# Attention on one core: transposes of q, k and the log rows in the half-array form of the scores, and one PSUM slot for both halves of the product with v

## The chip, the cores and the metric

One core of a Trainium2 chip runs the whole program. The metric is the device time of one launch in microseconds (us), taken as the median of repeated runs. The core has five engines with queues of their own: PE (TensorE, matrix products), DVE (VectorE), ACT (ScalarE), POOL (GpSimd) and SP, which here only starts transfers. Products land in PSUM, which DVE and ACT read; POOL can't. All data of the attention are single precision; a number is split into a high part of type fp32r and the rest, and products are made of the parts.

## What is computed

The reference chains an attention with decay and two expert layers. The change lies in the attention alone:

```python
B, H, S, D = q.shape                     # 4, 8, 576, 64
scores = scale * np.matmul(q, k.transpose(0, 1, 3, 2))
log_f = np.log(np.clip(f, 0.0001, 1.0))
cum = np.cumsum(log_f, axis=-1)
decay = cum[:, :, :, None] - cum[:, :, None, :]
scores = np.where(causal, -1000000000.0, scores + decay)
attn = np.exp(scores - np.max(scores, axis=-1, keepdims=True))
attn = attn / (np.sum(attn, axis=-1, keepdims=True) + 1e-09)
x = np.matmul(attn, v)                   # then moe (w_in, w_out), then moe2 (gate, w1, w2)
```

## The kernel before

**Stages.** The first stage is the attention of 32 heads, worked as 16 pairs of heads; weights of w_in are loaded and converted beside it. Then come the products with w_in and w_out (`h`, `acc`), the routing, and eight experts (`h`, `y`). The stage of attention runs from the start to the first product `h<-X,wh`.

**One pair.** `prepare` loads q and k of a pair (tiles `x3`, and `x4` for the last 64 tokens), transposes them on PE into a PSUM tile `s`, and ACT and DVE make the high parts (`qh`, `kh`) and low parts (`ql`, `kl`); here lines 636 to 665. `offsets` multiplies all parts for scores with queries along the partitions, finds each row's minimum of the negated scores (DVE, `kept`, `nm`), sums the exponentials (ACT, `sm`), makes the logarithm of the sums (ACT, then a series on POOL, tile `ln`) and turns maximum plus logarithm into rows by a transpose (`rows`, line 676; ACT and DVE split it, tile `xr`; SP carries it into `qr`). `attend` multiplies again with keys along the partitions, takes exponentials that are then final (`P`), zeroes what is not causal (POOL, `affine_select`), multiplies with v in two halves of the queries (`values`, 320 and 256 columns) and stores the result as high and low parts (`finish`, tile `xt`).

**Forms of PE.** The products of the scores use rows 0 to 63 for one head and rows 64 to 127 for the other, side by side ("64*128" in the rows). Products with v use columns in two halves ("128*64"). Transposes and the products with the weights use the whole array ("128*128").

**Who sets the order.** `Plan` holds every operation with its engine, an assumed length in ns, what it needs, a rank, and the buffers that it takes; `order` runs through the plan as a list of events and so fixes the order of each engine. The ranks are `12 * n` plus constants (`ZP`, `ZO`, `ZA`, `ZS`, `ZH`, `ZL`, `ZR`) and a table by pair (`ZN`, `ZM`, `ZB`). On PE it looks for another ready operation of the same `form` (within `NEAR` ranks) before it changes form, which it counts with `TURN` (200 ns). PSUM has four slots `s` (`SB`), each of two banks of 512 words. All operations recorded so have line 72 in the profile.

Of the kernel before, what the change touches and what calls it, by code (L numbers as in the profile page):

```python
# [37 lines left out]
ZX = 500  # L38
ZP, ZO, ZA, ZH, ZL, ZW, DW = -39, -27, 5, -9.5, -10.5, 63, 14.5
ZS = 5, 5.5, 7, 0.5, 2.5, 11, 11.5  # L40
ZQ = 1
ZT = 0, 7
ZR = 5.5
MW = 1.5, 0.6
# [6 lines left out]
NEARB = 5  # L51
ZN = 0.5, 0, -4, 0, 0, 0, -0.5, 0, 0, 0, 0, 0, 0, 0, 2, 0.5
ZM = -2.5, -0.5, 0, -1, 0, 0, 0, 0, 0, 0, 0, 1, -1.5, 0.5, 4, -4
ZB = 0, -4, -5, 0, 0, 0.5, -0.5, 0, 0, -3, 0, -4, 0.5, 0, 0, -1
NK = 4
# [36 lines left out]
class Plan:  # L92
# [4 lines left out]
           ("vec", "act"): 205, ("vec", "gp"): 155, ("act", "gp"): 180}  # L97
    MOVE = 650, 2600
    TURN = 200
# [4 lines left out]

    def op(self, eng, ns, fn, needs=(), rank=0.0, takes=(), uses=(), move=0, plain=False, form="A"):
        o = Op(eng, ns, fn, [x for x in needs if x is not None], rank)
        o.move, o.form = move, form
# [12 lines left out]
        self.ops.append(o)  # L120
        return o
# [4 lines left out]
    def order(self):  # L126
# [100 lines left out]
def tile_kernel(ctx, tc, q, k, v, f, w_in, w_out, w_gate, w1, w2, out):  # L227
# [35 lines left out]
    def weight_ops(op, pieces, z, st, low_on, keep=None, hold=()):  # L263
# [7 lines left out]
        def chunk(c, src):  # L271
# [32 lines left out]
            wb = o.got[0]  # L304
            s = op("gp", 800, square, [o], z, ["wsq"], [wb])
            sq = s.got[0]
# [3 lines left out]
            o = op("vec", 335, b2, [o], z, (), [bb, wb])  # L310
            s = op("gp", 816, big, [s], z, (), [sq])
            takes = [] if "b" in st else ["wst"]
            o = op("gp", 687, mul, [s, o] + st.get("o", []), z, takes, [sq, bb] + ([st["b"]] if "b" in st else []))
            if takes:
# [198 lines left out]
    with ExitStack() as c1:  # L513
# [63 lines left out]
        QO = stp.tile([128, 128], FR, name="qo")  # L577
        VT = [stp.tile([128, 5, 2, D], FT, name=f"vt{i}") for i in range(2)]
        pads = []
        for n in range(NS):  # L580
# [16 lines left out]
            if n < 2:  # L597
                op("gp", 150, lambda n=n: gp.memset(VT[n][64:, 4], 0.0), (), 12 * n - 90)
        marks, users = [], []
        heads = [(b, hp) for b in range(B) for hp in range(H // 2)]  # L600

        def prepare(n, own, z):
# [30 lines left out]
            def part(end, z):  # L633
                mine = {}

                def flip():
                    mine[0] = p = bank()
                    if end:
                        pe.transpose(p[:, 0, :128], x3["end"].rearrange("p s d -> p (s d)"), ident)
                        return  # L640
                    for j in range(2):
                        for t in range(4):
                            pe.transpose(p[:, j, 128 * t:128 * t + 128], x3[j][:, t].rearrange("p s d -> p (s d)"), ident)

                def high(j, c0, w, a):
                    hi = (qh[:, 64:] if j else kh)[:, c0:c0 + w]
                    x = mine[0][:, 0, a:a + w] if end else mine[0][:, j]
                    if j:
# [4 lines left out]
                def low(j, c0, w, a):  # L653
                    hi, lo = ((y[:, 64:] if j else y)[:, c0:c0 + w] for y in ((qh, ql) if j else (kh, kl)))
                    x = mine[0][:, 0, a:a + w] if end else mine[0][:, j]
                    vec.scalar_tensor_tensor(lo, x, 0.125 if j else 1.0, hi, op0=OP.mult, op1=OP.subtract)
                if end:
                    o = op("pe", 109, flip, loads["end"], z, ["s"], buf["end"] + list(sets.values()))
# [4 lines left out]
                for j, c0, w, a in ([(0, 512, 64, 0), (1, 512, 64, 64)] if end else [(0, 0, 512, 0), (1, 0, 512, 0)]):  # L663
                    a_ = op("act", 51 + .833 * w, lambda x=(j, c0, w, a): high(*x), [o], z + ZH, (), [tb, sets[j]])
                    outs[j] += [a_, op("vec", 69 + 1.042 * w, lambda x=(j, c0, w, a): low(*x), [a_], z + ZL, (), [tb, sets[j]])]
            part(False, z)
# [9 lines left out]
        def rows(x, dst, need, z, uses, duse):  # L676
# [3 lines left out]
            def flip():  # L680
                mine[0] = bank()[:10, 0, :128]
                pe.transpose(mine[0], x(), ident)

            def high():
                mine[1] = at.tile([10, 2, 128], FR, name="xr", tag="xr", bufs=2)
                act.copy(mine[1][:, 0], mine[0])

            def low():
                vec.tensor_tensor(mine[1][:, 1], mine[0], mine[1][:, 0], op=OP.subtract)
            o = op("pe", 107, flip, need, z + 1, ["s"], uses)  # L690
            st = o.got[0]
# [5 lines left out]
        def offsets(n, own, z):  # L697
# [70 lines left out]
            def ratio():  # L768
                own["ln"] = x = at.tile([128, 4, 10], FT, name="ln", tag="ln", bufs=2)
                act.activation(x[:, 0], own["sm"].bitcast(I32), AF.Copy, scale=LN[0], bias=LN[1])  # L770
                act.activation(x[:, 1], x[:, 0], AF.Exp)

            def ready():
                x = own["ln"]
                gp.tensor_scalar(x[:, 3], own["sm"], 1e-9, None, op0=OP.add)

            def series():
                x, t = own["ln"][:, 2], own["ln"][:, 1]
                gp.tensor_tensor(t, own["ln"][:, 3], t, op=OP.mult)
                gp.tensor_scalar(x, t, LN[5], LN[4], op0=OP.mult, op1=OP.add)  # L780
# [3 lines left out]
                gp.tensor_scalar(x, x, LN[2], None, op0=OP.add)  # L784
                gp.tensor_tensor(x, x, own["ln"][:, 0], op=OP.add)
# [3 lines left out]
            p = op("gp", 250, ready, tots + [o], z + ZR, (), [sb, lb])  # L789
            o = op("gp", 2200, series, [o, p], z + ZR, (), [nb, sb, lb])  # L790
            own["max"] = rows(lambda: own["ln"][:, 2], lambda l: qr[32 + l:97 + l:64], [o], z + ZR, [lb], kq)

        def attend(n, own, z):
# [18 lines left out]
            def score(name, blocks, z):  # L812
# [24 lines left out]
                for n, (i, f0, f1) in enumerate(blocks):  # L837
                    sel = []
                    if f0 == 128 * i:
                        w = min(128, f1 - f0)  # L840
                        sel = [op("gp", 137 + 1.75 * w, lambda a=col[n], w=w: causal(a, w), acts, z + 4, (), [pb])]
                    for half, (q0, w) in enumerate(HALF):
# [4 lines left out]
            def values(half, i, z):  # L847
                need, pb, name, a, e, x, y = W[half, i]

                def product():  # L850
                    if i == 0:
                        own["av", half] = bank()[:, 0]
                    for u in range(2):
                        pe.matmul(own["av", half][64 * u:64 * u + 64, x:y], own["v"][:, i, u], own["P", name][:, u, a:e],
                                  start=i == 0, stop=i == (2, 4)[half])
                o = op("pe", 4 * (e - a) / 2.4 + 12, product, need + vl + R.get(("av", half), []), z, ["s"] if i == 0 else [],
                       [vb, pb] + R.get(("avb", half), []), form="V")
                if i == 0:
                    R["avb", half] = [o.got[0]]
                R["av", half] = [o]  # L860

            def finish(half, z):
# [22 lines left out]
                if rest == "gp":  # L885
                    o = op("gp", 96 + 3.55 * w, lambda: low(1), [o], z + 1, (), [xb])
                    o = op("gp", 148 + 2.1 * w, lambda: low(0), [o], z + 1, (), [xb])
                else:
# [534 lines left out]
```

## Time and profile before

| | before |
|---|---|
| median of 3 runs (lowest, highest) | 925.02 us (924.19, 928.3) |
| profiled execution, its span | 927.42 us, 925.7 us |
| busy: PE, DVE, ACT, POOL | 889.4, 584.0, 416.6, 457.6 us |
| from 40 to 180 us: PE, DVE, ACT, POOL | 137.07, 103.50, 130.83, 108.47 us |
| granted clock of PE over the span | 0.989 |

Busy time of PE counts the modelled ends of pipelined products, so lengths of PE are read from start to start. A row of the timeline merges alike instructions ("x8") and gives the start of the first. A wait is put down to the engine whose signal came last.

### The profile page before, as it was taken

The numbers are of one execution on the slowest core, as the hardware profiler recorded it, in microseconds if no ns is written. First come the engines' busy times: TensorE is split into PE (matmuls) and PEld (weight loads), VectorE is DVE, ScalarE is ACT, GpSimd is POOL, SyncE is SP. The second block draws the span as 40 slices with busy tenths as digits, with TensorE's granted clock in tenths as the row PEclk, the third lists the DMA queues.
The fourth block names the chain that finished last, engine by engine and source line by source line (L and its number), as shares of the span: only waits on it lengthen the run. The fifth ranks groups of instructions, "written<-read, shape, count | busy, mean of one in ns | idle before, by whom it ended". The sixth has DMA issues, their size and how long they took to land.

```text
span 925.7 us, 19093 instructions
## 1 busy us (share of the span) xinstructions
PE 889.4 (96%) x6934; PEld 755.8 (82%) x6934; DVE 584.0 (63%) x1439; ACT 416.6 (45%) x983; POOL 457.6 (49%) x683
## 2 busy tenths in 40 slices
PE   6899999998999999999999999999899999999996
PEld 6688878876877787777777777777689999999996
DVE  8778876517798389323576677766755665556631
ACT  7899999842222233223122222222344555455521
POOL 8588895548997078000645655555662122121101
PEclk9899999999999999999899999999999999999999
DMA  6566654559984384321312212211246765656611
GB/s 128 149 163 172 182 138 120 178 148 339 323 281 148 137 261 134 114 82 46 124 48 70 69 46 69 69 58 58 80 163 190 225 189 177 196 186 194 189 38 35
DMA packets 139967, 132.36 MB, mean 143 GB/s; under 512 B 68480, under 2 KB 106688, under 8 KB 139872
## 3 DMA queue, kind: packets, MB, share of 16 engines
q1 hardware_dynamic: 135600, 121.40, 42.5%
q0 software_dynamic: 3072, 9.44, 3.5%
q8 instruction: 55, 0.90, 0.4%
q10 hardware_dynamic: 1200, 0.30, 0.1%
q14 instruction: 40, 0.33, 0.1%
HBM read 99.84 MB, written 31.08 MB: 141 GB/s over the span
## 4 chain that ended last, share of the span: by engine, by line
PE 69%; issue 11%; POOL 10%; DVE 4%; ACT 2%; DMA 2%; SPq 0%; POOLq 0%; DVEq 0%; ACTq 0%
PE acc L1059 21%; PE h L72 19%; PE s L72 9%; PE h L1141 6%; PE y L1154 6%; POOL wsq L72 3%; PE T L72 3%; PE q_ct L1059 2%; POOL wst L72 2%; POOL ln L72 1%; ACT kept L72 1%; DVE r_ge L1301 1%; DVE kept L72 1%; POOL P L72 1%; POOL out L1162 1%
## 5 line engine op out<-in xcount | busy, mean ns | idle before, releaser
L72 PE MATMUL h<-X,wh 128*128 128x512 f32 (+1 forms) x960 | 209.6, 375 | 0.6 <-DVE xt L72 0.6
L72 PEld LDWEIGHTS h<-X,wh 128*128 128x128 f32 x960 | 165.0, 188 | 37.8 <-DVE g L72 2.7
L1059 PE MATMUL acc<-wh,gh 128*128 128x512 f32 x576 | 188.2, 404 | 0.0
L453 POOL TENSOR_TENSOR gl<-g,gh 128x512 fp32r<-128x512 f32 x64 | 104.9, 1643 | 82.7 <-ACT gh L452 73.9
L1059 PEld LDWEIGHTS acc<-wh,gh 128*128 128x128 f32 x576 | 108.1, 192 | 19.3
L359 ACT CAST wh<-wst 128x512 fp32r<-128x512 f32 x132 | 80.4, 621 | 84.6 <-DMA wst<-in_moe_w 49.4
L1059 PE MATMUL acc<-wh,gl 128*128 128x512 f32 x288 | 117.4, 408 | 0.9 <-POOL gl L453 0.9
L1141 PE MATMUL h<-XE,wh 128*128 128x288 f32 x768 | 116.7, 301 | 0.9 <-DVE XE L1003 0.9
L72 DVE TENSOR_TENSOR wh<-wst,wh 128x512 fp32r<-128x512 f32 x132 | 91.2, 713 | 40.3 <-ACT wh L359 28.1
L452 ACT CAST gh<-g 128x512 fp32r<-128x512 f32 x72 | 44.5, 621 | 155.0 <-PE acc L1059 132.5
L72 ACT ACTIVATE g<-h 128x512 f32<-128x512 f32 (+1 forms) x80 | 44.4, 555 | 154.4 <-PE h L72 154.4
L1141 PEld LDWEIGHTS h<-XE,wh 128*128 128x128 f32 x768 | 105.3, 189 | 1.2 <-DVE XE L1003 1.2
L1154 PE MATMUL y<-eh,wh 128*128 128x288 f32 x512 | 98.3, 296 | 0.0
L72 DVE TENSOR_TENSOR g<-g,h 128x512 f32<-128x512 f32 (+1 forms) x80 | 50.2, 629 | 68.6 <-ACT g L72 68.2
L72 ACT ACTIVATE kept<-kept,nm 128x192 f32<-128x192 f32 (+4 forms) x160 | 88.0, 553 | 2.9 <-DVE nm L72 2.9
L1162 POOL DMA_INDIRECT out<-yo,ids x24 | 24.8, 1034 | 127.0 <-DVE yo L1161 117.9
L1154 PEld LDWEIGHTS y<-eh,wh 128*128 128x128 f32 x512 | 79.7, 188 | 0.0
L72 DVE SCALAR_TENSOR_TENSOR wbits<-w,wbits 128x256 int32<-128x256 int32 x128 | 76.2, 597 | 3.0
L72 DVE CUSTOM_DVE_ANT_0 kept<-s,mask 128x192 f32<-128x192 f32 (+4 forms) x160 | 59.2, 426 | 23.0 <-PE s L72 22.5
L1154 PE MATMUL y<-el,wh 128*128 128x288 f32 x256 | 68.2, 296 | 0.0
L72 POOL TENSOR_TENSOR wst<-wsq,wbits 128x256 f32<-128x256 f32 x64 | 49.6, 775 | 36.4 <-DVE wbits L72 31.5
L1059 PEld LDWEIGHTS acc<-wh,gl 128*128 128x128 f32 x288 | 55.3, 192 | 10.9 <-POOL gl L453 1.3
(228 smaller groups left out, 1594.9 us busy)
## 6 DMA issues: line engine op xcount, KB each, us to landing
wst<-in_moe_w SPq DMA_DIRECT2D x128, 256.0 KB
X<-xd SPq DMA_DIRECT2D x12, 1024.0 KB
g<-gd SPq DMA_DIRECT2D x36, 256.0 KB
w<-in_moe_w_in SPq DMA_DIRECT2D x32, 256.0 KB
w<-in_moe_w_out SPq DMA_DIRECT2D x32, 256.0 KB
gd<-g SPq DMA_DIRECT2D x16, 512.0 KB
xd<-xt SPq DMA_DIRECT2D x16, 320.0 KB
x2d<-xo SPq DMA_DIRECT2D x20, 256.0 KB
```

The source lines that it names most:

```text
L72: r = getattr(self.engine, name)(*a, **k)
L359: A.copy(r[u][0], x)
L452: A.copy(gh, g)
L453: on.tensor_tensor(gl, g, gh, op=OP.subtract)
L1059: tc.keep_in_program_order(PE.matmul(*a, **k))
L1141: PE.matmul(h[:, :CAP], w, X[:, c, x, :], start=n == 0, stop=n == 3 * NC - 1)
L1154: PE.matmul(yt[c][:, :CAP], w[:, s], a, start=j == 0 and n == 0, stop=j == NJ - 1 and n == 2)
L1162: sd = G.indirect_dma_start(out=out[:, :], out_offset=bass.IndirectOffsetOnAxis(ap=ids[:, 3 * e + t:3 * e + t + 1], axis=0), in_=y, in_off ...
L1301: V.scalar_tensor_tensor(many[:, :NT * (K + 1)].rearrange("p (i k) -> p i k", k=K + 1)[:, :, :K], key[:, :, None].to_broadcast(s), base if ...
```

## The change

q and k are loaded with four neighbouring tokens in each partition, and each transpose is made in two halves of 64 rows by 64 columns which write two banks of the slot; the rows of ln likewise, from a wider zeroed tile. Such transposes have the scores' form `S`, and `pull=False` keeps the plan from drawing them forward for the sake of the form. Each copy and subtraction of q and k now reads both banks, so the two copies (q first) and the two subtractions follow each other. The halves of the product with v take the two banks of one slot. The first half's result is copied by DVE instead of ACT (`FIN`). The ranks, the tables by pair and some assumed lengths have other numbers.

```diff
-ZP, ZO, ZA, ZH, ZL, ZW, DW = -39, -27, 5, -9.5, -10.5, 63, 14.5
+ZP, ZO, ZA, ZH, ZL, ZW, DW = -43.5, -24.5, 7, -3.5, -8.5, 61.5, 23.5
...
-FIN = ("act", "vec"), ("vec", "gp")
+FIN = ("vec", "vec"), ("vec", "gp")
...
-    MOVE = 650, 2600
+    MOVE = 650, 2200
...
-                    same = [x for x in q if x[2].form == form and x[0] <= q[0][0] + self.near]
+                    same = [x for x in q if x[2].form == form and x[0] <= q[0][0] + self.near * x[2].pull]
...
+        lnt = [stp.tile([128, 160], FT, name=f"ln{i}") for i in range(2)]
+        LNS = [{0: x[:, 0:10], 1: x[:, 10:20], 3: x[:, 20:30], 2: x[:, 32:42], 4: x[:, 32:160]} for x in lnt]
...
-                at_q[j].dma_start(x3[j][:, :, i], src[b, h + i, :512].rearrange("(t p) d -> p t d", p=128))
+                at_q[j].dma_start(x3[j][:, :, i], src[b, h + i, :512].rearrange("(p t) d -> p t d", t=4))
...
-                    for j in range(2):
-                        for t in range(4):
-                            pe.transpose(p[:, j, 128 * t:128 * t + 128], x3[j][:, t].rearrange("p s d -> p (s d)"), ident)
+                    for j, t in [(0, 0)] if end else [(j, t) for j in range(2) for t in range(4)]:
+                        for r in range(2):
+                            d = slice(64 * r, 64 * r + 64)
+                            if end:
+                                pe.transpose(p[:, r, :64], x3["end"][d].rearrange("p s d -> p (s d)"), ident[d, d])
+                            else:
+                                pe.transpose(p[:, r, 4 * j + t::8], x3[j][d, t].rearrange("p s d -> p (s d)"), ident[d, d])
...
+                    return mine[0].rearrange("p r (c n) -> p (r c) n", n=8)[:, :, 4 * j:4 * j + 4]
...
-                    o = op("pe", 872, flip, loads[0] + loads[1], z, ["s", "k", "q"], buf[0] + buf[1])
+                    o = op("pe", 888, flip, loads[0] + loads[1], z, ["s", "k", "q"], buf[0] + buf[1], form="S", pull=False)
...
+                for j in (1, 0):
+                    need = [o] if end or j else [o, a_[1]]
+                    a_[j] = op("act", 51 + .833 * w, lambda x=(j, c0, w, 0): high(*x), need, z + ZH, (), [tb, sets[j]])
+                for j in range(2):
+                    need = [a_[j]] if end else list(a_.values())
...
                 def product():
+                    if i == 0 and half == 0:
+                        own["avs"] = bank()
                     if i == 0:
-                        own["av", half] = bank()[:, 0]
+                        own["av", half] = own["avs"][:, half]
```

On PE, around one product with v in the middle of the stage, stood before (`x_112` and `x_113` are k and q of a later pair, `x_2331` their last 64 tokens):

```order
L72 MATMUL s<-kl_132,qh_128 128x288 x2
L72 MATMUL s<-kr_133,qo 128x288 x2
L72 MATMUL s<-ident,ln 10x128
L72 MATMUL s<-ident,x_112 128x128 x4
L72 MATMUL s<-ident,x_113 128x128 x4
L72 MATMUL s<-P,vt_135 64x320 x2
L72 MATMUL s<-P,vt_135 64x192 x2
L72 MATMUL s<-P,vt_135 64x64 x2
L72 MATMUL s<-P,vt_135 64x256 x6
L72 MATMUL s<-P,vt_135 64x192 x2
L72 MATMUL s<-P,vt_135 64x64 x2
L72 MATMUL s<-ident,x_2331 128x128
```

The same place on PE, with the change:

```order
L72 MATMUL s<-kl_132,qh_128 128x288 x2
L72 MATMUL s<-kr_133,qo 128x288 x2
L72 MATMUL s<-P,vt_135 64x320 x2
L72 MATMUL s<-P,vt_135 64x192 x2
L72 MATMUL s<-P,vt_135 64x64 x2
L72 MATMUL s<-P,vt_135 64x256 x6
L72 MATMUL s<-P,vt_135 64x192 x2
L72 MATMUL s<-P,vt_135 64x64 x2
L72 MATMUL s<-ident,x_2379 128x64 x2
L72 MATMUL s<-ident,ln_137 128x64 x2
L72 MATMUL s<-qh_116,kh_119 128x320 x2
```

The transposes of k and q have gone from between the scores and v into the scores before (they stand some rows further up), the one of ln behind v, and no instruction of the whole array is left.

On POOL, between the store of one pair's result (`xt`) and the selects of the next (`AFFINE_SELECT`), stood before, in one of these places:

```order
L72 TENSOR_SCALAR ln<-sm 128x10
L72 TENSOR_SCALAR xt<-xt 128x256
L72 TENSOR_TENSOR ln<-ln 128x10
L72 TENSOR_SCALAR ln<-ln 128x10
L72 TENSOR_TENSOR ln<-ln 128x10
L72 TENSOR_SCALAR ln<-ln 128x10
L72 TENSOR_TENSOR ln<-ln 128x10
L72 TENSOR_SCALAR ln<-ln 128x10
L72 TENSOR_TENSOR ln<-ln 128x10
L72 TENSOR_TENSOR ln<-ln,nm 128x10
L72 TENSOR_TENSOR xt<-xt 128x256
L72 AFFINE_SELECT P<-P 128x2x128
```

and with the change:

```order
L72 TENSOR_SCALAR xt<-xt 128x256
L72 TENSOR_SCALAR ln_137<-sm 128x10
L72 TENSOR_TENSOR xt<-xt 128x256
L72 AFFINE_SELECT P<-P 128x2x128
L72 TENSOR_TENSOR ln_137<-ln_137 128x10
L72 TENSOR_SCALAR ln_137<-ln_137 128x10
L72 TENSOR_TENSOR ln_137<-ln_137 128x10
L72 TENSOR_SCALAR ln_137<-ln_137 128x10
```

The first select of a pair, on which its product with v waits, has moved ahead of the series for ln.

## Rows read from the trace of the kernel before

**Rows 1.** The page: busy time by engine, and its DMA line.

```profile
PE 889.4 (96%) x6934; PEld 755.8 (82%) x6934; DVE 584.0 (63%) x1439; ACT 416.6 (45%) x983; POOL 457.6 (49%) x683
DMA packets 139967, 132.36 MB, mean 143 GB/s; under 512 B 68480, under 2 KB 106688, under 8 KB 139872
```

**Rows 2.** Busy time by stretches, with the columns' names first.

```profile
core 0: us, PE busy (x) PEld busy (x) DVE busy (x) ACT busy (x) POOL busy (x), PEclk, DMA share, GB/s
27.60:30.90 3.30, 3.21 (x24) 3.20 (x25) 2.73 (x15) 3.30 (x15) 1.27 (x6) 0.50 0.59 132
41.20:44.50 3.30, 3.30 (x22) 2.09 (x20) 2.64 (x6) 2.28 (x7) 2.22 (x3) 0.50 0.61 138
40.00:180.00 140.00, 137.07 (x1675) 119.70 (x1677) 103.50 (x419) 130.83 (x393) 108.47 (x247) 0.99 0.57 152
```

**Rows 3.** Timeline of PE, one period: start us, us, line, operation, tiles, shape, count.

```profile
144.85 2.94 PE L72 MATMUL s<-P,vt 128*64 128x320 f32 x32
147.72 0.33 PE L72 MATMUL s<-ident,x 128*128 128x128 f32 x1
147.98 0.41 PE L72 MATMUL s<-qh,kh 64*128 64x320 f32 x2
...
152.38 0.28 PE L72 MATMUL s<-kh,ql 64*128 64x64 f32 x2
152.49 0.28 PE L72 MATMUL s<-kl,qh 64*128 64x64 f32 x2
...
154.52 0.29 PE L72 MATMUL s<-kl,qh 64*128 64x288 f32 x2
154.65 0.29 PE L72 MATMUL s<-kr,qo 64*128 64x288 f32 x2
154.88 0.28 PE L72 MATMUL s<-ident,ln 128*10 128x128 f32 x1
154.99 1.04 PE L72 MATMUL s<-ident,x 128*128 128x128 f32 x8
155.95 0.76 PE L72 MATMUL s<-P,vt 128*64 128x320 f32 x4
```

**Rows 4.** Timeline of PE near the end of the stage.

```profile
191.59 0.28 PE L72 MATMUL s<-qr,kr 64*128 64x64 f32 x2
191.80 2.96 PE L72 MATMUL s<-P,vt 128*64 128x320 f32 x32
194.69 0.41 PE L72 MATMUL s<-qh,kh 64*128 64x320 f32 x2
```

**Rows 5.** PE's waits, 10 to 40 us, then 40 to 202: total, times, longest.

```profile
PE s L72 <- DVE nm L72: 1.9, 4, 1.1
...
PE s L72 <- DVE xr L72: 2.0, 1, 2.0
PE s L72 <- POOL P L72: 1.7, 3, 1.3
```

**Rows 6.** Groups by shape, 0 to 202 us: busy us, mean ns; idle before, releaser.

```profile
L72 ACT ACTIVATE qh<-s 128x512 fp32r<-128x512 f32 x12 | 7.0, 585 | 0.0
L72 ACT CAST xt<-s 128x320 fp32r<-128x320 f32 x16 | 6.5, 408 | 2.7 <-PE s L72 2.7
...
L72 DVE SCALAR_TENSOR_TENSOR kl<-s,kh 128x512 fp32r<-128x512 f32 x12 | 8.3, 690 | 9.3 <-ACT qh L72 9.3
L72 DVE TENSOR_TENSOR xt<-s,xt 128x320 fp32r<-128x320 f32 x16 | 7.8, 485 | 9.8 <-ACT xt L72 9.8
L72 DVE COPY xt<-s 128x256 f32<-128x256 f32 x16 | 6.7, 418 | 3.6 <-PE s L72 3.1 <-issue 0.4
L72 DVE TENSOR_SCALAR wbits<-w 128x256 int32<-128x256 int32 x16 | 5.9, 367 | 4.4 <-DMA w<-in_moe_w_in 2.9 <-POOL wst L72 1.4
```

**Rows 7.** Timelines where attention ends, PE and POOL.

```profile
201.70 11.50 PE L72 MATMUL h<-X,wh 128*128 128x512 f32 x48 [0.58 <-DVE xt L72]
...
209.92 0.72 POOL L72 TENSOR_TENSOR wsq<-w 128x256 f32<-128x256 f32 x1 [6.52 <-DMA w<-in_moe_w_out]
```

More of the change, by code (lines that the diff above doesn't have):

```diff
@@ L103, in __init__, with op @@
         self.near, self.linger = near, linger
-    def op(self, eng, ns, fn, needs=(), rank=0.0, takes=(), uses=(), move=0, plain=False, form="A"):
+    def op(self, eng, ns, fn, needs=(), rank=0.0, takes=(), uses=(), move=0, plain=False, form="A", pull=True):
         o = Op(eng, ns, fn, [x for x in needs if x is not None], rank)
-        o.move, o.form = move, form
+        o.move, o.form, o.pull = move, form, pull
         for t in takes:
@@ L304, in chunk @@
             wb = o.got[0]
-            s = op("gp", 800, square, [o], z, ["wsq"], [wb])
+            s = op("gp", 665, square, [o], z, ["wsq"], [wb])
             sq = s.got[0]
@@ L310, in chunk @@
             o = op("vec", 335, b2, [o], z, (), [bb, wb])
-            s = op("gp", 816, big, [s], z, (), [sq])
+            s = op("gp", 875, big, [s], z, (), [sq])
             takes = [] if "b" in st else ["wst"]
-            o = op("gp", 687, mul, [s, o] + st.get("o", []), z, takes, [sq, bb] + ([st["b"]] if "b" in st else []))
+            o = op("gp", 740, mul, [s, o] + st.get("o", []), z, takes, [sq, bb] + ([st["b"]] if "b" in st else []))
             if takes:
@@ L637, in flip, with turned, like @@
                     mine[0] = p = bank()
-                    if end:
-                        pe.transpose(p[:, 0, :128], x3["end"].rearrange("p s d -> p (s d)"), ident)
-                        return
-                    for j in range(2):
-                        for t in range(4):
-                            pe.transpose(p[:, j, 128 * t:128 * t + 128], x3[j][:, t].rearrange("p s d -> p (s d)"), ident)
+                    for j, t in [(0, 0)] if end else [(j, t) for j in range(2) for t in range(4)]:
[5 more added lines that the diff above has]
+                                pe.transpose(p[:, r, 4 * j + t::8], x3[j][d, t].rearrange("p s d -> p (s d)"), ident[d, d])
+                def turned(j):
+                    if end:
+                        return mine[0][:, j, :64]
+                    return mine[0].rearrange("p r (c n) -> p (r c) n", n=8)[:, :, 4 * j:4 * j + 4]
+                def like(x):
+                    return x if end else x.rearrange("p (c t) -> p c t", t=4)
                 def high(j, c0, w, a):
-                    hi = (qh[:, 64:] if j else kh)[:, c0:c0 + w]
-                    x = mine[0][:, 0, a:a + w] if end else mine[0][:, j]
+                    hi, x = like((qh[:, 64:] if j else kh)[:, c0:c0 + w]), turned(j)
                     if j:
@@ L653, in low @@
                 def low(j, c0, w, a):
-                    hi, lo = ((y[:, 64:] if j else y)[:, c0:c0 + w] for y in ((qh, ql) if j else (kh, kl)))
-                    x = mine[0][:, 0, a:a + w] if end else mine[0][:, j]
+                    hi, lo = (like((y[:, 64:] if j else y)[:, c0:c0 + w]) for y in ((qh, ql) if j else (kh, kl)))
+                    x = turned(j)
                     vec.scalar_tensor_tensor(lo, x, 0.125 if j else 1.0, hi, op0=OP.mult, op1=OP.subtract)
                 if end:
-                    o = op("pe", 109, flip, loads["end"], z, ["s"], buf["end"] + list(sets.values()))
+                    o = op("pe", 111, flip, loads["end"], z, ["s"], buf["end"] + list(sets.values()), form="S", pull=False)
                 else:
-                    o = op("pe", 872, flip, loads[0] + loads[1], z, ["s", "k", "q"], buf[0] + buf[1])
+                    o = op("pe", 888, flip, loads[0] + loads[1], z, ["s", "k", "q"], buf[0] + buf[1], form="S", pull=False)
                     sets[0], sets[1] = own["k"], own["q"] = o.got[1:]
                 tb = o.got[0]
-                for j, c0, w, a in ([(0, 512, 64, 0), (1, 512, 64, 64)] if end else [(0, 0, 512, 0), (1, 0, 512, 0)]):
-                    a_ = op("act", 51 + .833 * w, lambda x=(j, c0, w, a): high(*x), [o], z + ZH, (), [tb, sets[j]])
-                    outs[j] += [a_, op("vec", 69 + 1.042 * w, lambda x=(j, c0, w, a): low(*x), [a_], z + ZL, (), [tb, sets[j]])]
+                a_ = {}
+                for j in (1, 0):
+                    c0, w = (512, 64) if end else (0, 512)
+                    need = [o] if end or j else [o, a_[1]]
+                    a_[j] = op("act", 51 + .833 * w, lambda x=(j, c0, w, 0): high(*x), need, z + ZH, (), [tb, sets[j]])
+                for j in range(2):
+                    need = [a_[j]] if end else list(a_.values())
+                    outs[j] += [a_[j], op("vec", 69 + 1.042 * w, lambda x=(j, c0, w, 0): low(*x), need, z + ZL, (), [tb, sets[j]])]
             part(False, z)
@@ L680, in flip @@
             def flip():
-                mine[0] = bank()[:10, 0, :128]
-                pe.transpose(mine[0], x(), ident)
+                p = bank()
+                for r in range(2):
+                    d = slice(64 * r, 64 * r + 64)
+                    pe.transpose(p[:, r, :64], x()[d], ident[d, d])
+                mine[0] = p[:10, :, :64]
             def high():
                 mine[1] = at.tile([10, 2, 128], FR, name="xr", tag="xr", bufs=2)
-                act.copy(mine[1][:, 0], mine[0])
+                act.copy(mine[1][:, 0].rearrange("p (r c) -> p r c", r=2), mine[0])
             def low():
-                vec.tensor_tensor(mine[1][:, 1], mine[0], mine[1][:, 0], op=OP.subtract)
-            o = op("pe", 107, flip, need, z + 1, ["s"], uses)
+                hi, lo = (mine[1][:, l].rearrange("p (r c) -> p r c", r=2) for l in range(2))
+                vec.tensor_tensor(lo, mine[0], hi, op=OP.subtract)
+            o = op("pe", 111, flip, need, z + 1, ["s"], uses, form="S", pull=False)
             st = o.got[0]
@@ L784, in series @@
                 gp.tensor_scalar(x, x, LN[2], None, op0=OP.add)
-                gp.tensor_tensor(x, x, own["ln"][:, 0], op=OP.add)
+                gp.tensor_tensor(x, x, own["ln"][0], op=OP.add)
                 gp.tensor_tensor(x, x, own["nm"][:, :10], op=OP.add)
@@ L788, in offsets @@
             lb = o.got[0]
-            p = op("gp", 250, ready, tots + [o], z + ZR, (), [sb, lb])
-            o = op("gp", 2200, series, [o, p], z + ZR, (), [nb, sb, lb])
-            own["max"] = rows(lambda: own["ln"][:, 2], lambda l: qr[32 + l:97 + l:64], [o], z + ZR, [lb], kq)
+            p = op("gp", 285, ready, tots + [o], z + ZR, (), [sb, lb])
+            o = op("gp", 1760, series, [o, p], z + ZR, (), [nb, sb, lb])
+            own["max"] = rows(lambda: own["ln"][4], lambda l: qr[32 + l:97 + l:64], [o], z + ZR, [lb], kq)
         def attend(n, own, z):
@@ L840, in score @@
                         w = min(128, f1 - f0)
-                        sel = [op("gp", 137 + 1.75 * w, lambda a=col[n], w=w: causal(a, w), acts, z + 4, (), [pb])]
+                        sel = [op("gp", 200 + 1.68 * w, lambda a=col[n], w=w: causal(a, w), acts, z + 4, (), [pb])]
                     for half, (q0, w) in enumerate(HALF):
@@ L855, in product @@
                                   start=i == 0, stop=i == (2, 4)[half])
[L856 to L859, printed above, removed]
+                o = op("pe", 4 * (e - a) / 2.4 + 12, product, need + vl + R.get(("av", half), R.get("begun", [])), z, ["s"] if i == half == 0 else [],
+                       [vb, pb] + R.get(("avb", 0), []), form="V")
+                if i == half == 0:
+                    R["avb", 0] = R["avb", 1] = [o.got[0]]
+                    R["begun"] = [o]
                 R["av", half] = [o]
```

31 lines of the change are left out of this document (16 added, 15 removed).

## Prediction, made before the changed kernel ran

> **What bounds the kernel now.** I read the page first: PE is busy 96% of the span, ACT, DVE and POOL 45 to 63% [rows 1]. The change sits in the attention stage, which ends with the first product with w_in at 201.7 us [rows 7]; so the second view is the table by stretches of that stage. From 40 to 180 us PE is busy 137.1 of 140 us, ACT 130.8, POOL 108.5, DVE 103.5 [rows 2]: two engines are nearly full at once, PE first. In two stretches, 27.6 to 30.9 and 41.2 to 44.5 us, the granted clock is 0.50, the lower of the two levels (1.2 GHz); both come behind waits of PE for DVE, of 1.1 us at the longest between 10 and 40 us and of 2.0 us just after [rows 2, 5]. The third view is one period of the pipeline on PE, from a product with v to the next, 144.85 to 155.95 us: 11.10 us without a wait [rows 3]. It goes V (products with v), one transpose, scores, nine transposes (one of ln, eight of q and k), V. The fourth is the list of PE's waits, of which the largest are in rows 5. What comes behind the stage hangs on it: the w_out loads stand on SP's queue behind the last stores of attention but one, and POOL waits for them until 209.92 us [rows 7]. So I let what the stage gains pass whole to the end.
>
> **Turns of PE (removed).** The scores use the array as two halves of 64 rows; the transposes of before use all of it (128x128); V uses two halves of columns. By the two orders of PE, up to the first product with w_in, PE changes form 64 times before and 34 times after. What a turn costs is read as start to start [rows 3, 4]. Between score pairs of 64 columns the step is 0.11 us (152.38 to 152.49), of 288 columns 0.13 us (154.52 to 154.65); between whole transposes 0.11 us (154.88 to 154.99).
> - V, one transpose, scores: from the transpose to the first score 0.26 us (147.72 to 147.98). V straight to scores takes as long from V's start to the next instruction as V to the transpose (2.89 us, 191.80 to 194.69, against 2.87 us, 144.85 to 147.72). So a transpose among the scores, at 0.11 us, saves 0.15 us. There are 9 such places: 1.35 us.
> - Scores, transposes, V: from score to transpose 0.23 us where 0.13 is the pace, so 0.10; from the last of eight transposes to V 0.96 - 7 x 0.11 = 0.19, so 0.08 over the pace. Scores straight to V: 0.21 us (191.59 to 191.80), 0.10 over. The saving is 0.10 + 0.08 - 0.10 = 0.08 us, at 12 places: 0.95 us.
> - Scores, transposes, scores: 4 places ahead of the first V, 0.10 + 0.15 = 0.25 us each, 1.0 us. PE waits for others there, so I count half, 0.5 us.
> Together 2.8 us, on the path since PE is 98% busy from 40 to 180 us.
>
> **The transposes themselves.** Each whole one becomes two of 64 rows by 64 columns. The trace has none of that kind; the nearest row is a score pair of 64 columns, which loads the same 64x128 weights twice and takes 0.11 us for both. That is the price of one whole transpose, so the swap costs nothing. The other end: the halves run one behind the other at 0.11 us each, 10 x 0.11 = 1.1 us for each of 16 head pairs, 17.6 us. I take the near row. Output with a stride of 8 words in PSUM, and ACT and DVE reading it in runs of four words, stand in no row; the nearest are DVE's copy of 256 neighbouring words from PSUM at 418 ns and its shift of 256 words of w, every second one, at 367 ns [rows 6]. By them a stride costs nothing, or gains 51 ns; I take nothing, and 51 ns either way for four copies and subtractions in 16 pairs, 3.3 us, as bounds.
>
> **ACT, DVE, POOL.** The copy of the first half of the result moves from ACT (408 ns, x16, 6.5 us) to DVE (about the 485 ns of the subtraction of the same size, 7.8 us) [rows 6]. ACT, 93% busy, becomes lighter by 0.41 us a period; DVE idles 36.5 of 140 us, 3.0 us a period, which hides the copy as long as it isn't at the head of DVE's queue when scores end. The subtraction for k now waits for both copies of ACT, q's first; a full copy is 585 ns. DVE already waits 9.3 us for ACT's copies of q ahead of the 12 subtractions for kl [rows 6], so I take nothing, and 0.59 us a pair, 7 us, as bound. On POOL the first causal select of a pair now stands ahead of the ln series instead of behind it, and the select is what V waited for (1.7 us in 3 places) [rows 5]; behind it now wait ln's series and its transpose, which have a period more. The ln transpose stands behind V instead of ahead of it, a period earlier than its user. One PSUM slot of four comes free during V; no wait of PE in rows 5 names a slot, so it is worth nothing by itself.
>
> The Trainium skill, page PSUM — Partial Sum Buffer, section PSUM bank collisions raise a hardware error, says that ScalarE and VectorE may not touch one bank and quadrant at once, reads against reads included. By it the two copies and two subtractions, which now share both banks, go one after another; that is the wait just named, and its price if nothing hid it would be the 7 us of the bound. The trace bears on it only so far as DVE waits for both copies already.
>
> **Loads.** q and k arrive as 1 KB per partition in a row instead of four runs of 256 B; 68480 of the kernel's 139967 packets are under 512 B [rows 1]. The DMA engines are 57% busy from 40 to 180 us [rows 2], and PE's waits are for DVE, POOL and ACT, not for loads. Taken as nothing, bound 0 to 1 us at the start.
>
> **PE's waits and the clock.** The waits for nm and xr, 1.9 and 2.0 us [rows 5], the 2.9 us that PE idles from 40 to 180 us [rows 2], and the two slow stretches (each 3.3 us and more at half speed, so some 3.4 us lost) make 10.2 us that could go. The order around V is looser (select earlier, ln earlier, ACT lighter), but it is another order, made from other numbers, and brings waits of its own. Between nothing (or as much again lost) and 10.2 us I take 3.1 us: one slow stretch (1.7) and half of the idle time from 40 to 180 us (1.4).
>
> **Sum.** 2.8 + 3.1 = 5.9 us. The profiled execution took 927.42 us around a span of 925.70; it would take 921.5. The median of the runs is 925.02, so 919.1; I write 919.0.
>
> **Rivals.**
> 1. *Only the turns pay.* PE's waits move but do not shrink, since ACT stays at over 90%. For: ACT's 130.8 of 140 us. Against: ACT loses 0.41 us in 11. Gain 1.5 to 3 us: 922.5.
> 2. *All waits go too.* The pipeline runs at its floor: one wait-free period is 11.10 - 0.15 - 0.08 = 10.87 us, and the ramp keeps the upper clock. For: several periods of before already have no wait. Against: ahead of the first V it is ACT that is full (3.30 of 3.30 us from 27.6 us on) [rows 2]. Gain 2.8 + 10.2 = 13 us at most, 10 at the least: 913.5.
> 3. *DVE becomes late* (slower). The second copy of ACT (0.59 us) and the moved copy (0.49 us) stand in one row on DVE's queue ahead of the next pair's maxima; behind them wait the exponentials of ACT, and PE's slots. It decides once waits use up the 3.0 us of slack a period. If 12 pairs pay 1.08 us, 13 - 2.8 = 10 us are lost: 935; if half, 3.7 us: 929.
> 4. *Halves don't overlap* (slower, the change doesn't do what it says): 17.6 - 5.9: 936.5. Against it stands the score pair of 64 columns.
>
> **How the numbers follow.** Forecast 0.50 (its own range 915 to 922), rival 1 0.25, rival 2 0.13, rival 3 0.08, rival 4 0.04. A measurement tells some 0.5%, 4.6 us: faster is under 920.4, slower over 929.6. Faster: four fifths of the forecast, rival 2, a little of rival 1, 0.57. Slower: rival 4, most of rival 3, 0.09. Same: the rest, 0.34. The range takes in rival 1, most of rival 2 and the milder rival 3: 911 to 928.
>
> **What would show it.** PE's order in the trace after: no 128x128 transposes before the first w_in product; a pair of half transposes every 0.11 us (0.22 for rival 4); a wait-free period of 10.9 us; the first w_in product near 196 us. ACT's share in 40 to 180 us falls to some 90%, DVE's rises from 74 to about 80%. Rival 3 would show as PE or ACT waiting for DVE's kl, ql or nm. I am wrong if PE's idle time from 40 to 180 us stays at 2.9 us or grows, or if the slow clock comes in more than two stretches.

## The result, and the profile after

The changed kernel takes 941.61 us (median of 4 runs, 941.35 to 944.09), the kernel before 926.66 us on the same chip (4 runs). The ratio is 1.0148, 95% interval 1.0113 to 1.0183: slower by 1.5%, where 919.0 us and a range of 911 to 928 us were predicted. The profiled span is 939.6 us.

The whole loss is made in the attention. The first product with w_in comes 13.2 us later than before and POOL's step behind the w_out load 12.3 us later [rows 7]; the span ends 13.9 us later. From the timeline of PE, after (start us, us, then the instruction):

```profile
214.88 1.43 PE L72 MATMUL h<-X,wh 128*128 128x512 f32 x5
```

And from that of POOL:

```profile
222.17 0.72 POOL L72 TENSOR_TENSOR wsq<-w 128x256 f32<-128x256 f32 x1 [4.94 <-DMA w<-in_moe_w_out]
```

That is 214.88 instead of 201.70 us; from there to the end of the span 724.7 us pass (before 724.0). So the first view is again the table by stretches; its columns are those of [rows 2].

```profile
41.20:44.50 3.30, 1.81 (x16) 0.55 (x14) 3.03 (x7) 3.30 (x12) 3.13 (x8) 1.00 0.61 167
40.00:180.00 140.00, 128.23 (x1716) 108.52 (x1712) 108.02 (x416) 126.86 (x380) 110.27 (x245) 1.00 0.54 148
```

PE idles 11.8 of 140 us, where it idled 2.9. No other engine has become full, and the clock is not at fault: the slow stretch of before is at 1.00. PE's waits say for whom it idles (total, times, longest), from 40 to 180 us:

```profile
PE s L72 <- DVE xt L72: 8.6, 11, 1.5
PE s L72 <- POOL P L72: 1.3, 3, 0.5
```

From 180 to 215 us the same list begins:

```profile
PE s L72 <- DVE xt L72: 4.9, 8, 0.7
```

The page's group of all products with v (busy, mean ns; idle time before them and what ended it) has both together:

```profile
L72 PE MATMUL s<-P,vt 128*64 128x256 f32 (+3 forms) x512 | 53.3, 342 | 16.0 <-DVE xt L72 13.6
```

`xt` is the result of the product with v, copied out of PSUM. In before no product with v waited for it. Its 13.6 us, in 11 places up to 180 us and 8 behind, are about the whole loss. One period on PE shows the place (to be read against [rows 3]):

```profile
150.00 2.50 PE L72 MATMUL s<-P,vt 128*64 128x320 f32 x24
153.23 0.66 PE L72 MATMUL s<-P,vt 128*64 128x192 f32 x8 [0.73 <-DVE xt L72]
153.82 0.28 PE L72 MATMUL s<-ident,x 64*128 64x64 f32 x2
...
159.94 0.73 PE L72 MATMUL s<-ident,x 64*128 64x64 f32 x16
160.46 0.41 PE L72 MATMUL s<-kh,qh 64*128 64x288 f32 x2
...
161.72 0.49 PE L72 MATMUL s<-P,vt 128*64 128x320 f32 x2
```

From V to the transpose behind it 3.82 us pass (150.00 to 153.82), before 2.87 us (144.85 to 147.72): PE stops in the middle of its own series, ahead of the last eight products. DVE at the same time (its timeline):

```profile
152.00 0.68 DVE L72 SCALAR_TENSOR_TENSOR ql<-s,qh 128x512 fp32r<-128x512 f32 x1
152.60 0.48 DVE L72 CAST xt<-s 128x320 fp32r<-128x320 f32 x1
153.93 0.49 DVE L72 TENSOR_TENSOR xt<-s,xt 128x320 fp32r<-128x320 f32 x1 [0.84 <-PE s L72]
```

PE's product of the second half waits until DVE has copied the first half (152.60 to 153.08), and DVE's subtraction for the first half waits 0.84 us for that product of the second half. Neither needs the other's data: the halves lie in two banks. The list of PE's instructions, which names what each waits for and holds no times, has the first of these waits, PE's for DVE, in the program itself. The product of the second half that follows the copy in the planned order reads, after and before:

```
L72 MATMUL s<-P,vt_135 64x192 [waits DVE_49,Pool_49]

L72 MATMUL s<-P,vt_135 64x192 [waits Pool_49]
```

So **theory S**, which the experiments below test: both halves are now one tile (`own["avs"]`, one slot of two banks), and the framework keeps writes and reads of one tile in program order, whichever part they touch. The plan knows nothing of that: to it the halves are independent, so it puts the reads of the first half in between the products of the second.

### The profile page after: what moved, and what is told of

Its sections match the earlier page's. It is cut to its first block, busy times and chain, and to the rows that moved or that the text cites. A ratio compares the mean times of both kernels' runs of the same rounds, so it can differ in the third digit from the quotient of the medians.

```text
span 939.6 us, 19322 instructions
## 1 busy us (share of the span) xinstructions
PE 885.7 (94%) x7094; PEld 746.7 (79%) x7094; DVE 589.8 (63%) x1455; ACT 412.9 (44%) x967; POOL 459.3 (49%) x685
## 4 chain that ended last, share of the span: by engine, by line
PE 66%; issue 12%; DVE 9%; POOL 8%; DMA 3%; ACT 1%; SPq 0%; POOLq 0%; DVEq 0%; ACTq 0%
PE acc L1082 21%; PE h L72 15%; PE s L72 11%; PE h L1164 6%; PE y L1177 6%; PE T L72 2%; DVE wbits L72 2%; PE q_ct L1082 2%; POOL wsq L72 2%; DVE r_ge L1324 2%; DVE xt L72 1%; DVE kept L72 1%; POOL out L1185 1%; POOL wst L72 1%; POOL xt L72 1%
## 5 line engine op out<-in xcount | busy, mean ns | idle before, releaser
L72 DVE SCALAR_TENSOR_TENSOR wbits<-w,wbits 128x256 int32<-128x256 int32 x128 | 73.3, 574 | 3.0
L72 PE MATMUL s<-P,vt 128*64 128x256 f32 (+3 forms) x512 | 53.3, 342 | 16.0 <-DVE xt L72 13.6
```

The source lines that it names most:

```text
L72: r = getattr(self.engine, name)(*a, **k)
```

## Experiments

**The slot undone, in two ways (e1, e2).** e1 keeps the order and gives each half a tile of its own (the scores' ring has three slots left); e2 gives each half a slot of the four, planned anew.

```diff
+ e1
-            return ps.tile([128, 2, 512], FT, name="s", tag="s", bufs=SB)
+            return ps.tile([128, 2, 512], FT, name="s", tag="s", bufs=SB - 1)
...
-                    if i == 0 and half == 0:
-                        own["avs"] = bank()
-                        own["av", half] = own["avs"][:, half]
+                        own["av", half] = ps.tile([128, 512], FT, name=f"av{half}", tag=f"av{half}", bufs=1)
+ e2
-                        own["av", half] = own["avs"][:, half]
+                        own["av", half] = bank()[:, 0]
...
```

> The changed kernel with its order of instructions kept, but the two halves of the product with v are two PSUM tiles of one bank each, and the scores have a ring of three slots. Theory S (the shared tile is ordered as one: a product for the second half waits until DVE has copied the first half out, and DVE's subtraction waits for the second half's products): PE's 13.6 us of waits for DVE xt in front of V go, the period falls from 11.7 to some 10.9 us, and the time from 941.6 to 922-930 us. Rival O (the new order is worse, whatever the tile): the waits come back under other names and the time stays at 936 us or more. Rival L (the copy moved to DVE is late): time stays above 935 us.

> The changed kernel with each half of the product with v in a slot of its own, as in the kernel before; the order is planned anew with the changed numbers. Theory S: no wait of V for DVE xt, 920-930 us. Rival O: 936 us or more.

Measured: e1 939.55 us (ratio 1.0146, 1.0124 to 1.0168), e2 939.48 us (1.0158, 1.0135 to 1.0181). Both miss theory S's range and lie where rival O had put them: no gain, though the wait for `xt` inside V is gone in both. PE's waits from 40 to 180 us in e1:

```profile
PE s L72 <- DVE ql L72: 4.0, 6, 0.8
PE s L72 <- DVE nm L72: 3.4, 12, 0.3
PE s L72 <- DVE X L72: 2.3, 3, 1.0
```

And in e2:

```profile
PE s L72 <- DVE xt L72: 6.9, 11, 1.5
PE s L72 <- POOL ln L72: 3.0, 3, 2.2
```

Now it is scores and transposes that wait, in e2 for a slot out of which `xt` is still being read, as its timeline of PE shows:

```profile
149.08 0.41 PE L72 MATMUL s<-qh,kh 64*128 64x320 f32 x2 [0.56 <-DVE xt L72]
...
150.12 0.47 PE L72 MATMUL s<-qh,kh 64*128 64x448 f32 x2 [0.18 <-DVE xt L72]
```

Part of e1's loss lies ahead of the first V, which comes at 47.60 us (after 40.25). From 25 to 40 us its granted clock is 0.51, near the lower level, where after's is 1.00 from 10 to 180 us; just ahead of that PE waits 2.2 us for `ql`. The row of e1:

```profile
25.00:40.00 15.00, 13.45 (x106) 12.23 (x106) 9.08 (x46) 9.52 (x38) 2.24 (x10) 0.51 0.33 75
```

That a slot is now held until two copies and two subtractions of q and k are done in a row, and that slots are short for this reason, is an argument that no run here tests by itself. These two runs don't decide on theory S, since each also takes a slot away from the scores.

**One part added to the kernel before (e3, e4).** e3 is before with the shared slot alone; every engine keeps the order that it has in before. e4 is before with the halved transposes, their loads, the wide ln tile and q copied ahead of k, but before's slots, copy of the result and numbers.

```diff
+ e3
-                        own["av", half] = bank()[:, 0]
+                    if i == 0 and half == 0:
+                        own["avs"] = bank()
+                        own["av", half] = own["avs"][:, half]
...
+ e4
...
-                            pe.transpose(p[:, j, 128 * t:128 * t + 128], x3[j][:, t].rearrange("p s d -> p (s d)"), ident)
+                                pe.transpose(p[:, r, 4 * j + t::8], x3[j][d, t].rearrange("p s d -> p (s d)"), ident[d, d])
...
```

> The kernel before with the one change that both halves of the product with v share a slot. Theory S: a wait of some 0.7 us in each of 16 products with v and twice that in the last four, 12 to 15 us: 937-942 us. Rival O and rival L: no slower than before, 924-929 us, since neither the numbers nor the copy are changed.

> The kernel before with the transposes of q, k and ln in halves and the loads that go with them, and nothing else: slots, ranks, lengths and the copy by ACT as before. Theory S says that this part is a gain: turns 2.8 us, and a pair of halves takes 0.066 us in the changed kernel where a whole transpose takes 0.11, ten per head pair, 16 pairs, 7 us, less what the late start costs (first scores 4.7 us later in the changed kernel): 915-925 us. If the halves themselves are the loss: 930 us or more.

Measured: e3 951.29 us (ratio 1.0283, 1.0261 to 1.0306); e4 953.76 us (1.0294, 1.0269 to 1.0319). PE's waits from 40 to 180 us in e3:

```profile
PE s L72 <- DVE xt L72: 6.7, 9, 0.8
PE s L72 <- ACT xt L72: 5.8, 11, 0.5
PE s L72 <- DVE xr L72: 2.0, 1, 2.0
```

And in e4:

```profile
PE s L72 <- ACT P L72: 6.9, 10, 1.7
PE s L72 <- POOL ln L72: 3.6, 5, 1.0
```

The slot alone brings the wait for `xt` into V in the kernel before, where it never stood, and costs it 25 us, with the order of every engine unchanged. Theory S had the direction right and the size wrong: 12 to 15 us were expected. In most periods V takes 4.57 us from its start to the next instruction, 1.7 us more than before's 2.87, where a wait of 0.7 us had been reckoned with. e4 missed theory S's 915 to 925 us and lies on the other side, where the halves themselves would be the loss. Its waits are spread over many names, and its order was planned anew under numbers that were made for another plan. e8 below holds the halves too and shows no such loss, so e4 doesn't price the halves by themselves; how much of its 28 us is the plan wasn't taken apart.

**The order within the tile taken away (e8, e9).** e8 is the changed kernel, e9 is e3, both with each product of one half and each read of the other declared independent. Tiles, slots and the order of instructions stay. This needs no other data: the two halves never share a bank.

```diff
+            def apart(half, kind, o):
+                own.setdefault((kind, half), []).append(o)
+                for x in own.get(("r" if kind == "w" else "w", 1 - half), []):
+                    tc.declare_no_dep(o.ins, x.ins, reason="other bank")
... (called at each of these products, copies and subtractions)
```

> The changed kernel, with one thing more: the products with v of one half and the reads of the other half are declared independent (they lie in different banks). Same tiles, same four slots, same order of instructions. Theory S (the shared tile makes the second half's product wait for the reads of the first): the 13.6 us that PE waits for DVE's xt in the changed kernel go, the period falls from 11.7 to 10.6 to 11.0 us, the first product with w_in comes at 201 to 204 us instead of 214.9, time 927 to 931 us. Theory P (slots run short as soon as that wait is gone, as in e1 and e2): PE waits for ql, nm or X instead, 937 to 941 us. Theory N (the order of the changed kernel is simply not made for these waits): within 2 us of 941.6.

> The kernel before with the shared slot alone (as in e3, 951.3 us), with the two halves declared independent. Theory S (the order within one tile costs it all): back to 924 to 930 us, PE's waits for xt under 2 us from 40 to 180 us. Theory Z (what costs is that the slot of both halves is held longer, until the second half has been read): 943 to 951 us, since that stays as it was.

Measured: e8 927.51 us (ratio 1.0011, 0.9991 to 1.0032), e9 928.53 us (1.0029, 1.0003 to 1.0055). Against 1.0148 and 1.0283 this gives back 1.4% and 2.5% by one declaration, with the order of every engine unchanged: theory S stands, P (slots run short at once) and N fall, and Z (the slot is held longer) falls as the cause of the loss. The waits of PE from 40 to 180 us in e8:

```profile
PE s L72 <- POOL P L72: 4.1, 3, 2.0
PE s L72 <- DVE xt L72: 1.5, 4, 0.8
```

And in e9:

```profile
PE s L72 <- POOL P L72: 2.0, 3, 1.5
PE s L72 <- DVE xr L72: 1.8, 1, 1.8
```

The timeline of PE in e8, one period and the end of the stage:

```profile
145.66 2.94 PE L72 MATMUL s<-P,vt 128*64 128x320 f32 x32
148.53 0.28 PE L72 MATMUL s<-ident,x 64*128 64x64 f32 x2
...
149.19 0.31 PE L72 MATMUL s<-qr,kr 64*128 64x320 f32 x2
149.65 0.47 PE L72 MATMUL s<-qh,kh 64*128 64x448 f32 x2
...
156.48 0.49 PE L72 MATMUL s<-P,vt 128*64 128x320 f32 x2
...
200.79 2.38 PE L72 MATMUL h<-X,wh 128*128 128x512 f32 x9
```

DVE beside it in e8:

```profile
148.26 0.48 DVE L72 CAST xt<-s 128x320 fp32r<-128x320 f32 x1
148.77 0.49 DVE L72 TENSOR_TENSOR xt<-s,xt 128x320 fp32r<-128x320 f32 x1
149.18 0.41 DVE L72 COPY xt<-s 128x256 f32<-128x256 f32 x1
```

And its table of the stretch from 40 to 180 us:

```profile
40.00:180.00 140.00, 132.75 (x1814) 113.13 (x1812) 110.94 (x442) 132.06 (x399) 115.00 (x258) 1.00 0.57 158
```

V takes 2.87 us again (145.66 to 148.53), the subtraction follows the copy at once, and the first product with w_in comes at 200.79 us. A little of Z is left: the scores at 149.65 us start just behind the end of DVE's copy of the second half (149.18 and 0.41 us), which frees the slot of both halves; such waits make up the 1.5 us for `xt` in 4 places. e8 has the order of e1 and differs in the arrangement of the slots: a fourth one in the scores' ring is worth 12 us here (939.55 to 927.51), 7.3 us of it ahead of the first V (47.60 us in e1, 40.29 in e8). In before, without halved transposes, the freed slot brings nothing (e9).

**Other reasons for the loss (e5, e10).** e5 puts the first half's copy back on ACT; e10 is e8 with k copied first, as before.

```diff
+ e5
-FIN = ("vec", "vec"), ("vec", "gp")
+FIN = ("act", "vec"), ("vec", "gp")
+ e10, beside what e8 has
-                for j in (1, 0):
+                for j in (0, 1):
-                    need = [o] if end or j else [o, a_[1]]
+                    need = [o] if end or not j else [o, a_[0]]
```

> The changed kernel with the copy of the first half of the result on ACT again, as in the kernel before; replanned. Theory L (the copy is late on DVE, behind ql and nm, and with it xt, for which the second half waits): the copy on ACT frees the half sooner, PE's wait for xt falls by half or more, 930 to 935 us. Theory S (the wait is that of the tile's order, whoever reads): PE's waits for xt stay over 7 us from 40 to 180 us, 938 to 945 us.

> e8 with k's copy ahead of q's on ACT again, as in the kernel before. The changed kernel has its first scores at 15.1 us instead of 10.4, yet its first product with v at the same 40.25 us. Theory S says the start is recovered by then: within 1.5 us of e8. Theory T (the late start and the q-first order cost part of the loss all along): 3 to 5 us less than e8.

Measured: e5 943.57 us (ratio 1.0185, 1.0168 to 1.0203), e10 931.11 us (1.0047, 1.0027 to 1.0067). PE's waits in e5 from 40 to 180 us:

```profile
PE s L72 <- ACT xt L72: 6.0, 11, 0.6
PE s L72 <- DVE xt L72: 4.9, 8, 0.7
```

Whoever copies is waited for, so the engine isn't the cause, and theory L falls. e10 missed both expectations: it was to equal e8 or beat it by 3 to 5 us, and is 3.6 us slower, with waits for `xt` of 4.6 us from 40 to 180 us. Its order was planned anew, so it doesn't price the q-first order; it gives no sign that this costs time. Nor does the q-first order set the late start: in after as in e10 the first scores come at 15.08 us (before 10.37), and e4, with before's slots and numbers, has them at 14.98 us. So the late start comes with the halved transposes and their loads. The timeline of PE in after shows a wait for a load of q, which is over at 11.01 us, and then a longer one for `X`:

```profile
11.01 0.36 PE L72 MATMUL s<-ident,x 64*128 64x64 f32 x1 [1.78 <-DMA x<-in_q]
15.08 0.95 PE L72 MATMUL s<-X 64*128 64x192 f32 x6 [3.71 <-DVE X L72]
```

DVE, which makes the low parts in `X`, waits there for a transfer into the same tile:

```profile
13.64 1.42 DVE L72 SCALAR_TENSOR_TENSOR X<-s,X 128x512 fp32r<-128x512 f32 x3 [5.04 <-DMA X<-kept]
```

In before it starts at 8.93 us, behind 0.66 us of waiting for ACT. Whether this wait too is one of a tile's order alone wasn't tested.

By the first V after has caught up (40.25 us in both kernels); V to the next V then takes 14.9 us against 12.8, in e8 13.9. That may be the rest of the late start; it wasn't taken apart.

**What e8 still waits for (e11 to e14).** PE does less work per period than before, and e8 is no faster. Two answers: POOL's selects stand behind steps on the expert weights (e11 moves them ahead, e12 lets the plan prefer them), or ACT is full (e13 and e14 make it lighter in e8 and in before; they leave out part of the sums of exponentials, so they serve for the time alone).

```diff
+ e11, after the plan is made
+        if o.eng == "gp" and getattr(o, "select", False):
...
+            done.insert(n, done.pop(k))
+ e12
-                        sel = [op("gp", 200 + 1.68 * w, lambda a=col[n], w=w: causal(a, w), acts, z + 4, (), [pb])]
+                        sel = [op("gp", 200 + 1.68 * w, lambda a=col[n], w=w: causal(a, w), acts, z - 2, (), [pb])]
+ e13, e14
-                    x = sc["kept", u][:, :S] if i else sc["kept", u][:, a:a + c1 - c0]
+                    x = sc["kept", u][:, S - 128:S] if i else sc["kept", u][:, max(a, a + c1 - c0 - 128):a + c1 - c0]
```

> e8 with POOL's causal selects moved ahead of the steps on the expert weights (one of 0.7 to 2.5 us each) that stand right before them in POOL's order; PE's order is that of e8. Theory W (what PE saves in e8 is eaten by its three waits for POOL's selects, 4.1 us from 40 to 180 us): these waits fall under 1.5 us, the first product with w_in comes 2.5 to 4 us earlier than in e8 (200.8), at 197 to 198.5 us, time 923 to 925.5 us. Theory A (the waits only move: ln's rows, behind the selects on POOL, or the scores that wait for the slot, come late instead): within 1.5 us of e8's 927.5 us.

> e8 with the selects' rank lowered by 6, so that the planner takes them before whatever else POOL has ready, and plans the whole stage anew. Theory W: as e11, 922 to 926 us, waits for POOL's selects under 1.5 us. Theory A: 926 to 932 us, with other waits in their place.

> e8 with less work on ACT: the sums of exponentials (tile kept) are taken over the last 128 columns of a block alone, so the rest of the sum is left out. By e8's rows an instruction of 576, 448, 320 or 192 columns takes 770, 663, 549 or 448 ns and one of 128 about 395, so ACT gets lighter by some 1.7 us in each period; the order of PE, DVE and POOL is that of e8. Theory F (in e8 it is ACT that is full, 10.79 of 10.82 us in a period and 132 of 140 us, so that what PE saves comes back as its waits): the waits shrink, most periods come to 10.5 us, the first product with w_in moves from 200.8 to 194 to 197 us, and the time to 919 to 923 us. Theory G (the waits come from where selects and slots stand in the orders of POOL and DVE): the first product with w_in stays within 1.5 us of 200.8, time 926 to 929 us.

> The kernel before with the same work left out on ACT, as the other side of e13. Here PE is the fuller engine in the middle of the stage (a period of 11.10 us without a wait). Theory F: only the waits of before can go, 2 to 5 us at the first product with w_in (201.7), 921 to 925 us, and e13 comes out 2 to 5 us below this. Theory G: within 2 us of 926, and e13 no lower than this by more than 1 us.

Measured: e11 930.60 us (ratio 1.0025, 1.0000 to 1.0050), e12 927.89 us (0.9998, 0.9979 to 1.0017), e13 928.02 us (1.0000, 0.9982 to 1.0019), e14 928.95 us (1.0000, 0.9975 to 1.0026); before was at 927.65 us beside e11 and e12, at 928.18 us beside the other two. PE's waits in e11 from 40 to 200 us:

```profile
PE s L72 <- POOL ln L72: 2.4, 2, 1.9
PE s L72 <- POOL P L72: 2.4, 3, 1.0
PE s L72 <- DVE xt L72: 2.2, 6, 0.6
```

In e13 from 40 to 180 us:

```profile
PE s L72 <- POOL P L72: 3.8, 2, 2.0
PE s L72 <- DVE X L72: 2.4, 1, 2.4
```

And e13's table of that stretch:

```profile
40.00:180.00 140.00, 132.53 (x1824) 114.55 (x1824) 110.93 (x444) 114.36 (x405) 113.68 (x254) 1.00 0.59 161
```

In e11 the selects come earlier and `ln`, now behind them on POOL, is late instead: theory A's waits, though e11 is 3 us above e8, outside A's 1.5 us. In e12 the waits for the selects are 2.9 us and those for `xt` 2.8 us from 40 to 200 us: theory A again. In e13 ACT is busy 114.36 us instead of 132.06 us from 40 to 180 us, and the first product with w_in comes at 199.15 us, 1.6 us earlier than in e8: theory F (194 to 197 us) falls, in e14 as well, so a full ACT isn't what keeps e8 from being faster. G, that places in the orders of POOL and DVE set it, fits better, though its 1.5 us are just missed (PE still waits 2.0 and 1.8 us in two places for a select). It isn't shown: no run here took those waits away without putting others in their place. None of the twelve runs beats the kernel before.

## Why the prediction was wrong, step by step

- **The PSUM slot: the step that failed.** "No wait of PE in rows 5 names a slot, so it is worth nothing by itself" asked only what the freed slot would bring. What the edit adds was put at nothing without a row, a bound or a rival: a tile that two series of products and three reads use by turns. It costs some 14 us in the changed kernel (first product with w_in 214.88 against 200.79 us, 941.61 against 927.51 us) and 23 us in the kernel before (951.29 against 928.53 us). It could have been read ahead of time from the list of what PE's instructions wait for. The chance for slower, 0.09, went to two other mechanisms.
- **PE's waits and the clock, -3.1 us.** Failed as well, and by itself: with the false wait gone (e8) PE still idles 7.25 us from 40 to 180 us, more than the 2.9 us of before, of which half was to go. The two slow stretches did go (the row of 41.20 us above stands at 1.00). That looser places around V would shrink the waits didn't come true: e8, e11 and e12 have others in their stead.
- **Turns of PE and halved transposes.** Right in sign; the price of a pair of halves was too high. Eight pairs of halves take 0.52 us (159.94 to 160.46), 0.065 us a pair and not the 0.11 of the nearest row, a score pair of 64 columns; rival 4 is out. A period of e8 is 10.82 us (145.66 to 156.48), 0.28 us less than the 11.10 of before, with one wait for a slot in it (149.19 to 149.65, 0.46 us where the pace is 0.15); without that it would be 10.5 us, an estimate, where 10.87 was predicted. Most other periods of e8 hold waits as well. From the second V to the first product with w_in e8 takes 146.6 us (from 54.17), before 148.7 (from 53.02). So 2.1 us are gained there, where the turns alone were to bring 2.8 us, but the second V stands 1.1 us later, and in the time of the whole kernel no gain shows (ratio 1.0011).
- **k's subtraction behind both copies: nothing.** Right as far as the rows go. DVE's wait ahead of the 12 subtractions for `kl` falls from 9.3 us [rows 6] to the 0.4 us of this group of after (up to 215 us):

```profile
L72 DVE SCALAR_TENSOR_TENSOR kl<-s,kh 128x512 fp32r<-128x512 f32 x12 | 8.3, 688 | 0.4 <-ACT kh L72 0.4
```

  The reads out of PSUM with a stride cost nothing either: 688 ns against 690.
- **The copy on DVE: hidden.** e5 agrees as far as it goes; back on ACT nothing is gained. Rival 3 (DVE late) named `kl`, `ql` or `nm` as its sign. DVE is the engine in PE's waits, but for `xt`, and e5 shows that the tile and not the engine is waited for. That rivals 3 and 4 had the kernel slower is luck: neither mechanism came.
- **Loads.** The sum (nothing) holds to the first V, though the first scores come 4.7 us late, where 0 to 1 us was the bound. One statement fails: 1 KB in a row for q and k was read from the source side. The packets under 512 B are as many as before [rows 1] (after's line on the page), as the two heads still lie interleaved in `x3`, in runs of 256 B:

```profile
DMA packets 139966, 132.36 MB, mean 141 GB/s; under 512 B 68480, under 2 KB 106688, under 8 KB 139872
```

- **The gain of the stage passes whole to the end.** Held for the loss: 13.2 us at the first product with w_in, 13.9 us in the span.
- **The sentence "I am wrong if PE's idle time from 40 to 180 us stays at 2.9 us or grows"** named the sign that came.

## What to carry to other kernels

Two accumulators that share one tile are one thing to a framework that orders by tiles, even in separate banks: before costing an edit that merges buffers, list the reads and writes of the merged one in program order and look for a write that now follows a read of the other part, and read the semaphores in the instruction list. Tell the framework of the independence, or keep the reads of one half out of the writes of the other. And a planner whose model doesn't hold that order can place work where it hurts, as here the reads of the first half in between the products of the second.

## What the runs showed of the hardware

- A pair of half transposes of 64 rows and 64 columns takes 0.065 us (0.52 us for eight, 159.94 to 160.46 in after), against 0.11 us for a whole 128x128 one [rows 3]. That the two run side by side is an inference: one behind the other, at the whole one's pace per column, they would take 0.11 us again. No run timed a half alone.
- PE writing one bank of a slot while DVE reads the other shows no cost. In e8 DVE's copy of the first half starts at 148.26 us, beside V's last products, which go on to 148.53; V takes 2.87 us as in before [rows 3], and the copy 0.48 us as in after, where PE stood still beside it (152.60). The Trainium skill, page PSUM — Partial Sum Buffer, section PSUM bank collisions raise a hardware error, says that two engines on different banks run clean, so by it the wait was never needed; e8 agrees.
- An engine that is 94% busy need not bound (ACT in e8, 132.06 of 140 us): with 17.7 us of ACT's work left out from 40 to 180 us (e13, 114.36 us) the stage ended 1.6 us earlier.
